# Sliding-window attention with a feed-forward: keys and queries transposed by DMA from the fourth batch on, tokens loaded in pairs

## The chip, the cores and the metric

The kernel runs on one core of a Trainium2 chip. The metric is the time of one execution in microseconds (us), taken on the device. The kernel before takes 356.32 us, the median of three runs (355.86 to 357.08). "Faster" and "slower" mean by more than 2%. A profile is one execution: single places of a trace are given to tenths, but small differences between two traces should not be leant on.

Engines are named as the profile names them: PE is TensorE, PEld its weight loads, DVE is VectorE, ACT is ScalarE, POOL is GpSimd, SP is SyncE and SPq the queue of DMAs that SyncE issues.

## The reference, cut to what matters

```python
B, H, S, D = 8, 8, 576, 64                       # q, k, v: float32
scores = q @ k.transpose(0, 1, 3, 2) / np.sqrt(D)
mask = np.abs(pos[:, None] - pos[None, :]) <= 32  # window of 32 tokens to each side
attn = softmax(where(mask, scores, -1e9)) @ v
x = attn.transpose(0, 2, 1, 3).reshape(4608, 512)
h = x @ w_in                                      # 512 -> 2048
out = np.maximum(0.01 * h, h) @ w_out             # 2048 -> 512, float32
```

## The kernel before

The work is 64 attention steps: eight batches of 576 tokens, in each two halves of 288 queries, in each half four pairs of heads. Between the steps stand chunks of the feed-forward, which take the tokens that the steps have finished. In a step, PE makes the scores `ps` (five matmuls against the block-diagonal keys `kbd`), ACT the exponential, GpSimd multiplies by a mask (`pr`), PE makes the sums `s` and the weighted values `x`, and VectorE takes the reciprocal `r` of `s` and writes `xT = x * r`. In the traces each of these engines takes its work in the order of the program, so VectorE's key copies, output copies, reciprocals and multiplications stand in one line (in the changed kernel a reciprocal at 112.41 us comes behind a key copy that had waited 3.05 us).

Queries and keys are loaded as float32, cast to bf16, and turned by PE through an identity matrix, since the matmuls contract over the head dimension:

```python
RUN = S // 96                                   # six tokens = 1536 bytes in one run
def load_qk(b, p, behind=None):
    for into, src, name in ((qf, q, "qf"), (kf, k, "kf")):
        t = fload.tile([96, 2, RUN * D], FP32, name=f"{name}{p}")
        if behind is not None:                  # a tiny copy that must wait for a weight
            nc.sync.dma_start(out=t[0:1, 0, 0:1], in_=behind.bitcast(FP32)); behind = None
        nc.sync.dma_start(out=t, in_=src[b, p:H:NPAIR].rearrange("a (p c) d -> p a (c d)", c=RUN))
...
def transposes(b, first=False):                 # a piece for each of 4 pairs, q and k
    ...
            for c in range(RUN):
                nc.tensor.transpose(tp[:, c], src[:, p, c].rearrange("p a d -> p (a d)"), ident[0:96, 0:96])
            ...                                 # ACT copies tp to qT, or to kT and then:
                    for a in range(2):
                        r = slice(64 * a, 64 * a + 64)
                        nc.vector.tensor_copy(out=kbd[b % 2][r, p, :, r],
                                              in_=kT[r].rearrange("p (n j) -> p n j", j=64))
...
# start of batch 1, under the first feed-forward chunks
for p in range(NPAIR):
    load_qk(1, p, w_in_bf[0:1, 0, 512:514] if p == 0 else None)
...
for p in range(NPAIR):
    load_v(1, p, w_out_bf[0:1, 4, 0:2] if p == 0 else None)
for f in range(FFC):
    h_tile(256, 256, f)
    if f % 4 == 3:
        next(second); next(second)              # transposes of batch 1
        nc.gpsimd.memset(vbd[1][:, f // 4], 0.0)
score(8)
```

The tiny copy named `behind` makes the loads of batch 1 wait until a certain weight has landed, so that they do not take the queue from the weights.

The softmax here doesn't subtract the row's maximum and nothing guards it: scores larger than these inputs give would overflow.

## Time and profile before

| | before |
|---|---|
| median of 3 runs | 356.32 us |
| profiled span, granted clock | 353.9 us, 1.000 |
| PE / VectorE / ACT / GpSimd busy | 324.3 / 211.8 / 183.4 / 178.7 us |
| transposes on PE, whole program | 384 of 96 columns (192 for q, 192 for k) |
| copies of keys into `kbd` | 64, 28.4 us of VectorE |

Three lines of the page: SyncE's queue (packets, MB, share of the DMA engines), the chain that ended last by engine, and the sums on PE (busy us, mean ns, then the idle time before them and what ended it).

```profile
q1 hardware_dynamic: 56388, 37.76, 42.7%
...
PE 77%; DMA 7%; DVE 6%; POOL 4%; SPq 2%; issue 2%; ACT 1%; DVEq 0%; POOLq 0%; ACTq 0%
...
L238 PE MATMUL s<-pr,ones_bd 128*128 128x288 bf16 x64 | 19.0, 297 | 8.7 <-DVE r L252 7.0
```

PE makes 77% of the chain, and its waits for the reciprocal sum to 7.0 us. The kernel is a PE stream with a start of some 65 us ahead of it.

### The profile page before, as it was taken

How to read it: one execution, taken by the hardware profiler on the slowest of the kernel's cores; microseconds unless marked ns; L12 is line 12 of the kernel's file. 1: busy time of each engine (PE TensorE's matmuls, PEld its weight loads, DVE VectorE, ACT ScalarE, POOL GpSimd, SP SyncE). 2: the span in 40 equal slices, each digit the busy share in tenths (PEclk: the TensorE clock that was granted, in tenths of full speed). 3: DMA queues.
4: the chain of work that ended last, by engine and by line, in shares of the span. 5: the costliest groups of instructions: out<-in, count | busy, mean ns of one | idle time of the engine just before them, and what ended most of it. 6: DMA issues, size and time to landing. Idle time of an engine off the chain costs nothing.

```text
span 353.9 us, 6635 instructions
## 1 busy us (share of the span) xinstructions
PE 324.3 (92%) x2600; PEld 208.2 (59%) x2624; DVE 211.8 (60%) x242; ACT 183.4 (52%) x363; POOL 178.7 (51%) x213
## 2 busy tenths in 40 slices
PE   2658998999989898999999898999999999999995
PEld 1437864584957655656656555656656656555472
DVE  5588647757686877645653778554676676630101
ACT  5765862292845637518527527716528517326060
POOL 7797676578765766524543568533655423200000
PEclk9999999999999999999999999999999999999999
DMA  8999986599995274342453265340010010020101
GB/s 187 214 205 236 269 162 182 144 201 235 209 255 146 58 222 133 69 126 88 140 162 70 63 177 165 88 124 33 0 61 30 2 61 31 5 86 0 61 31 59
DMA packets 60707, 42.37 MB, mean 120 GB/s; under 512 B 39684, under 2 KB 56068, under 8 KB 60676
## 3 DMA queue, kind: packets, MB, share of 16 engines
q1 hardware_dynamic: 56388, 37.76, 42.7%
q0 software_dynamic: 4288, 4.20, 7.2%
q8 instruction: 20, 0.33, 0.4%
q14 instruction: 11, 0.09, 0.1%
HBM read 36.70 MB, written 9.44 MB: 130 GB/s over the span
## 4 chain that ended last, share of the span: by engine, by line
PE 77%; DMA 7%; DVE 6%; POOL 4%; SPq 2%; issue 2%; ACT 1%; DVEq 0%; POOLq 0%; ACTq 0%
PE mm L273 33%; PE mm L264 31%; DMA kf<-in_k_dram 7%; DVE r L252 5%; PE x L246 3%; PE tp L187 3%; PE ps L220 3%; PE s L238 2%; PE s L239 2%; SPq L71 1%; POOL vbd L175 1%; POOL vbd L400 1%; SPq L82 1%; DVE xT L254 1%; POOL pr L230 1%
## 5 line engine op out<-in xcount | busy, mean ns | idle before, releaser
L252 DVE RECIPROCAL r<-s 128x288 f32<-128x288 f32 x64 | 125.1, 1954 | 38.5 <-PE s L239 38.2
L230 POOL TENSOR_TENSOR pr<-e,mask 128x544 bf16<-128x544 bf16 x64 | 77.7, 1213 | 115.0 <-ACT e L226 114.7
L264 PE MATMUL mm<-xT,w_in_bf 128*128 128x384 bf16 (+1 forms) x896 | 132.7, 304 | 0.9 <-ACT kT L201 0.8
L268 ACT ACTIVATE gT<-mm 128x384 bf16<-128x384 f32 (+1 forms) x224 | 99.0, 445 | 63.0 <-PE mm L264 58.6
L273 PE MATMUL mm<-w_out_bf,gT 128*128 128x512 bf16 x552 | 126.8, 379 | 1.3
L264 PEld LDWEIGHTS <-w_in_bf 128*128 128x128 bf16 x896 | 86.6, 98 | 38.0 <-issue 1.3
L273 PEld LDWEIGHTS <-gT 128*128 128x128 bf16 x576 | 54.9, 98 | 61.1
L226 ACT ACTIVATE e<-ps 128x544 bf16<-128x544 f32 x64 | 39.8, 622 | 77.6 <-PE ps L220 77.6
L280 DVE COPY o_sb<-mm 128x512 f32<-128x512 f32 x36 | 24.9, 691 | 66.8 <-PE mm L273 66.8
L204 DVE COPY kbd<-kT 64x576 bf16<-64x576 bf16 x64 | 28.4, 444 | 18.2 <-ACT kT L201 17.6
L175 POOL CAST vbd<-vf 64x576 bf16<-64x576 f32 x58 | 38.3, 661 | 1.9
L254 DVE TENSOR_TENSOR xT<-x,r 128x288 bf16<-128x288 f32 x64 | 29.3, 458 | 7.0 <-PE mm L264 0.5
L165 POOL CAST kb<-kf 96x768 bf16<-96x768 f32 x32 | 26.6, 834 | 9.5 <-DMA kf<-in_k_dram 9.5
L246 PE MATMUL x<-pr,vbd 128*128 128x128 bf16 (+2 forms) x320 | 26.9, 217 | 2.0 <-POOL vbd L175 1.0
L220 PE MATMUL ps<-qT,kbd 128*128 128x128 bf16 (+2 forms) x320 | 27.3, 219 | 0.3
L238 PE MATMUL s<-pr,ones_bd 128*128 128x288 bf16 x64 | 19.0, 297 | 8.7 <-DVE r L252 7.0
L220 PEld LDWEIGHTS <-kbd 128*128 128x128 bf16 x320 | 21.1, 102 | 8.1 <-issue 0.6
L195 ACT ACTIVATE qT<-tp 128x576 bf16<-128x576 bf16 x32 | 20.8, 649 | 9.6 <-PE tp L187 9.0
L246 PEld LDWEIGHTS <-vbd 128*128 128x128 bf16 x320 | 21.4, 101 | 7.1 <-issue 2.8
L201 ACT ACTIVATE kT<-tp 128x576 bf16<-128x576 bf16 x32 | 20.8, 650 | 8.9 <-PE tp L187 7.9
L187 PE MATMUL tp<-ident,qb 96*128 96x96 bf16 x192 | 14.4, 214 | 8.5 <-DVE qb L165 6.7
L165 POOL CAST qb<-qf 96x768 bf16<-96x768 f32 x24 | 19.7, 820 | 0.0
(31 smaller groups left out, 107.7 us busy)
## 6 DMA issues: line engine op xcount, KB each, us to landing
qf<-in_q_dram SPq DMA_DIRECT2D x32, 288.0 KB, 3.5
kf<-in_k_dram SPq DMA_DIRECT2D x32, 288.0 KB, 3.9
vf<-in_v_dram SPq DMA_DIRECT2D x64, 144.0 KB, 3.4
out_dram<-o_sb SPq DMA_DIRECT2D x36, 256.0 KB, 2.2
w_in_bf<-in_moe_w_in_dram POOLq DMA_DIRECT2D x8, 256.0 KB, 6.4
w_out_bf<-in_moe_w_out_dram POOLq DMA_DIRECT2D x4, 512.0 KB, 13.5
qf<-w_in_bf SPq DMA_DIRECT2D x1, 0.0 KB
vf<-w_out_bf SPq DMA_DIRECT2D x1, 0.0 KB
```

The costliest lines, as they stand in the source:

```text
L165: eng.tensor_copy(out=dst[:, p], in_=src[b, p].rearrange("p a (c d) -> p c a d", d=D),)
L175: nc.gpsimd.tensor_copy(out=vbd[b % 2][r, p, :, r], in_=vf[b, p][r])
L204: nc.vector.tensor_copy(out=kbd[b % 2][r, p, :, r], in_=kT[r].rearrange("p (n j) -> p n j", j=64),)
L220: nc.tensor.matmul(ps[:, c0:c0 + n], kbd[b % 2][:, p, blk], qT[b][:, p, q0:q0 + n], start=True, stop=True,)
L226: nc.scalar.activation(out=e, in_=ps[:, 512 - HALF:512 - HALF + NCOL], func=AF.Exp, scale=scale,)
L230: nc.gpsimd.tensor_mul(pr, e, mask[hf])
L246: nc.tensor.matmul(x[:, a:a + n], vbd[b % 2][:, p, blk, :], pr[:, c0:c0 + n], start=(n_ == 0), stop=(n_ == len(WIN[hf]) - 1), skip_group_c ...
L252: nc.vector.reciprocal(r, s)
L254: nc.vector.tensor_mul(xT[:, p, t0:t0 + HALF], x, r)
L264: nc.tensor.matmul(h[:, 0:n], w_in_bf[:, c, ts(f, 128)], xT[:, c, ds(t0, n)], start=(c == 0), stop=(c == DMC - 1),)
L268: nc.scalar.activation(out=gT[t0][:, f, 0:n], in_=h[:, 0:n], func=AF.Prelu, alpha=0.01)
L273: nc.tensor.matmul(o, gT[t0][:, f, ts(j, 128)], w_out_bf[:, f, :], start=(f == 0), stop=(f == FFC - 1),)
```

## The change

The intent is to take 240 of the 384 transposes off PE, and the ACT copies behind them, and to give them to the DMA engines. For that the order of tokens had to change: a run is now two tokens (512 bytes), and inside a key block of 64 the 32 even tokens come first and the 32 odd ones after them. Masks, windows and the loads of values follow that order. The core of the diff, with cuts:

```diff
-    RUN = S // 96
+    RUN = 2
...
         for into, src, name in ((qf, q, "qf"), (kf, k, "kf")):
-            nc.sync.dma_start(out=t, in_=src[b, p:H:NPAIR].rearrange("a (p c) d -> p a (c d)", c=RUN))
+            for a in range(2):
+                if behind is not None:
+                    nc.sync.dma_start(out=t[0:1, a, 0, 0:1], in_=behind.bitcast(FP32))
+                nc.sync.dma_start(out=t[:, a],
+                    in_=src[b, NPAIR * a + p].rearrange("(m i c) d -> i m (c d)", i=NR, c=RUN))
...     # load_v: four loads for a tile in place of two, each behind a tiny copy where one is given
+    def place_keys(b, p):
+        t = kT.pop((b, p))
+        for a in range(2):
+            r = slice(64 * a, 64 * a + 64)
+            nc.vector.tensor_copy(
+                out=kbd[b % 2][r, p, :, r].rearrange("p n (c i) -> p n c i", c=RUN),
+                in_=t[r].rearrange("p (c n i) -> p n c i", c=RUN, n=NB))
...
+    def transpose_dma(b, p):
+        new_T(b, p)
+        for src, t in ((qb, qT[b][:, p]), (kb, kT[b, p])):
+            nc.sync.dma_start_transpose(out=t.rearrange("p (g i) -> p g i", i=NR),
+                                        in_=src[:, p].rearrange("p c m a d -> p (c m a d)"))
...     # weighted: s is made by five matmuls, block by block, in place of two
+    for b in range(2, B):
+        for p in range(NPAIR):
+            if b == 2:
+                i, j = (12, 13, 13, 14)[p], (14, 15, 15, 15)[p]
+                plan(13 + p, transpose_pe, b, p)
+            else:
+                i = 8 * (b - 1) + p
+                j = i + 4
+                plan(i + 3, place_keys, b, p)
+                plan(i + 1, transpose_dma, b, p)
+            plan(i, cast_qk, b, p)
+            plan(j, cast_v, b, p)
+            if b + 1 < B:
+                plan(i, load_qk, b + 1, p)
+                plan(j, load_v, b + 1, p)
```

The first three batches keep their transposes on PE. The second mask is now made after the first step instead of at the beginning.

## The prediction

> **What bounds the kernel now.** I read the page's engine shares and 40 slices first, then the chain of work that ended last, the PE timeline of the middle, the same timelines of the first 66 us, and the issues of the DMA queue there.
>
> ```profile
> PE 324.3 (92%) x2600; PEld 208.2 (59%) x2624; DVE 211.8 (60%) x242; ACT 183.4 (52%) x363; POOL 178.7 (51%) x213
> ...
> DMA  8999986599995274342453265340010010020101
> ```
>
> PE is far ahead of the rest, but a busy PE can still run below its rate, so I tested that. The chain in order of time, two stretches:
>
> ```profile
> 15.99 0.82 POOL kb L165
> ...
> 30.73 15.97 DMA kf<-in_k_dram
> 46.76 0.82 POOL kb L165
> 47.58 3.64 POOL vbd L400 x4
> ...
> 223.06 0.26 PE tp L187 x6
> ...
> 231.64 0.24 PE ps L220 x5
> ```
>
> The first column is the start, the second the time a piece adds. The upper lines are the start, where loads and POOL set the pace; the last two are from the middle, where the chain is PE alone. There, six transposes of 96 columns add 0.26 us, five score matmuls of 544 columns together add 0.24 us[...]. I gave every PE row of the timeline that cost and subtracted: from 140 to 200 us and from 220 to 340 us nothing is left over. The whole program's columns come to about 311 us; the other 43 us of the span are a start of about 18 us lost before 30 us, some 4 us at the end, and gaps of about 2 us where two attention steps follow each other without a feed-forward part between them:
>
> ```profile
> 215.91 0.42 PE L187 MATMUL tp<-ident,qb 96*128 96x96 bf16 x6
> 216.46 0.40 PE L220 MATMUL ps<-qT,kbd 128*128 128x64 bf16 x5
> 217.89 0.30 PE L238 MATMUL s<-pr,ones_bd 128*128 128x288 bf16 x1 [1.03 <-DVE r L252]
> ```
>
> So there are two regimes: the PE stream binds from about 65 us to the end, and any column removed there is time; up to about 65 us a chain of loads, casts and first steps binds, and any delay there is carried to the end undiminished, because no slack follows.
>
> [...] in the timeline the five score matmuls take 0.65 us before 28 us and 0.40 us afterwards, although the granted clock in the page is full throughout. [...] no run so far shows a transpose. [...] undisturbed packets of 256, 1536 and 2048 bytes take about 15 to 18, 65 and 82 ns.
>
> **The change part by part.**
> (a) Removed from PE: batches 3 to 7, 5 x 48 = 240 transposes of 96 columns, 240 x 42.5 ns = 10.2 us, all inside the stretch that is pure PE stream. Where two steps adjoin, the transposes had filled part of a wait on the reciprocal; about four such places lie in that range, and each loses about 0.25 us of the saving: -1.0. Net -9.2 us.
> (b) The sums of the probabilities become five matmuls instead of two, the same 544 columns: 3 x 2.5 ns x 64 = 0.5 us more. Key placing stays on DVE at 0.44 us x 64; mask multiply, exponential and reciprocal stay. The transposes no longer have one PSUM buffer but the four of the feed-forward: the one wait of 0.74 us for the copy of qT at 87 us goes. Together about -0.2.
> (c) ACT loses 40 copies of 0.65 us = 26 us. PE waited for ACT almost nowhere, so nothing follows on the path.
> (d) 40 DMA transposes of 96x768 bf16, 147 KB. [...] the 2 to 4 us to landing that loads show here. Keys are placed two steps (some 9 us) after, and needed at the earliest two steps after that. Hidden.
> (e) Loads. Queries and keys go from 12288 packets of 1536 bytes to 36864 of 512. From the packet records in the crowded start (about 30 ns for 256 bytes, 105 ns for 1536), an interpolated 45 ns for 512: three take 135 ns in place of 105. For one batch (4608 packets over 16 engines) that is 13.0 us in place of 10.1. Issues double as well: two per query or key tile, four per value tile, about 0.4 us each, and the issue order of the new program shows each waiting for the one eight before it.
>
> What (e) and the new masks cost, along the chain of the start:
> - The last keys of batch 0 landed at 15.99 us, and POOL was waiting for them (0.57 us idle). Up to 3 us later by (e). The second mask, five small copies on POOL, now stands ahead of the third step's mask multiply, which had 0.3 us to spare: 1 us more. Start: +2.5 to +4, say +3.
> - Batch 1: its loads are held back by one tiny copy out of the weights. Now there is one such copy ahead of each of the first two loads and of each of the first four value loads, and each load waits for its own to land:
>
> ```profile
> 22.77 0.73 SPq L69 DMA_DIRECT2D qf<-w_in_bf  x1
> 27.39 0.33 SPq L71 DMA_DIRECT2D qf<-in_q_dram  x1
> ...
> 38.24 0.62 SPq L80 DMA_DIRECT2D vf<-w_out_bf  x1
> 45.84 5.52 SPq L82 DMA_DIRECT2D vf<-in_v_dram  x8
> ```
>
> The first cost 4 us, the second 7 us, mostly in the queue behind the query and key loads. In the new program the value loads cannot begin before those are through, about 49 to 51 us by the shifts above; then three further rounds of load, tiny copy and landing, an estimated 2.5 to 3 us each from the shortest landings here (3.0 us for a value load): the first value tile is whole at about 60 to 62 us, is cast in 0.66 us, and the ninth step's value matmuls start about 62 us in place of here:
>
> ```profile
> 54.14 0.41 PE L246 MATMUL x<-pr,vbd 128*128 128x96 bf16 x5 [0.34 <-POOL vbd L175]
> ```
>
> That is +8 us at this point, in which the +3 of the start is contained. PE then stands still for some 5 us[...].
> Sum: -9.2 - 0.2 + 0.5 + 8 + 1 = +0.1. I take 356 us.
>
> **The rivals.**
> 1. The start hides it: the DMA engines keep working on the weights while the tiny copies wait, the weights then finish sooner, 512-byte packets cost nearer the undisturbed 25 ns (a line through 15 and 65 ns), and the value loads are done by 57. For it: the engines are busy nine tenths or more in most early slices, so no work is lost, only reordered. Against: the serial waits are latency, not bandwidth, and the first value cast already held PE for 0.34 us. Then 346 to 349 us.
> 2. The transposes are slow: if one takes 8 us or occupies the engines, eight per batch come to 64 us against some 42 us for eight steps, and the in-order queue of SyncE holds back loads and, behind them, output stores; DVE then stands before a full o_sb. For it: no trace here shows one, and SyncE now issues about twice as many DMAs. Against: [...] from 120 us on the DMA row shows 0.3 to 0.5 of capacity. Then 370 us and more.
> 3. The delay at the start is larger, each tiny copy taking the 4 to 7 us that it takes before: +6 to +10 more, about 363 to 366.
> 4. DVE becomes the bound where steps adjoin: without transposes between, the wait on the reciprocal (1.95 us) is bare. That is the 1 us in (a); DVE at 60% cannot bind elsewhere.
>
> **Range and chances.** The gain of 9 us is firm, the PE stream being accounted for to some tenths; the loss at the start has a spread of 3 to 12 us, and the transposes add a tail on the slow side. 356 us, 8 in 10 between 347 and 364. Faster by over 2% means below 349.2, so a start that loses under about 2.5 us: 0.25. Slower by over 2% means above 363.4: 0.17. Within: 0.58.
>
> **What would show it.** (a) right: from about 120 us no tp rows on PE, ACT some 26 us less busy, eight steps about 2 us shorter, and PE without gaps save at adjoining steps. (e) right: the value loads of batch 1 end at 62 us or later, and the ninth x waits several us for vbd, its start near 62 us; last keys of batch 0 land at 18 to 19 us. Wrong: an x at 57 us or before (rival 1), a kbd copy or a score in the middle that waits for a DMA, or o_sb copies that wait for stores (rival 2). The prediction falls if the first 65 us lose under 3 or over 15 us, or if PE shows waits on DMA after 120 us.

The sum came to +0.1 us; of its terms the last, +1 (a slower PE after its standstill), has lost its ground, and without it the sum is -0.9. The costs of 42.5 ns for a transpose and 2.5 ns for a further matmul in (a) and (b) can be had from the trace before: 32 matmuls of 256 columns take 3.49 us there (69.07 to 72.56) and 16 of 512 take 3.45 (207.53 to 210.98), so an estimate of 0.416 ns a column and 2.5 ns a matmul; 24 of 384 take 3.90, 162.5 ns each where the estimate gives 162.3, and the columns of the whole program come to the 311 us.

## The result, and the profile after

| | before | changed |
|---|---|---|
| median | 356.34 us (4 runs) | 360.73 us (4 runs, 359.88 to 362.08) |
| ratio | | 1.0125, 95% interval 1.0089 to 1.0161 |
| profiled span, granted clock | 353.9 us, 1.000 | 360.4 us, 0.995 |
| ACT busy | 183.4 us | 159.4 us |
| VectorE busy | 211.8 us | 224.2 us |

A ratio here and below is the mean time of one kernel's runs over the mean of the kernel before in the same rounds on the same chip, so it is not quite the ratio of the medians quoted. The outputs are right. The changed kernel is 1.25% slower: within 2%, 4.7 us above the predicted 356.0 and inside the range of 347 to 364. The total was near; two of its terms were not, and the rest of this text is about them.

The page of the changed kernel: engine shares, the busy tenths of PE and its granted clock in the 40 slices, SyncE's queue, the chain by engine, the sums on PE, and from the last part the two kinds of DMA transposes with their median time from issue to landing.

```profile
PE 316.3 (88%) x2552; PEld 202.5 (56%) x2576; DVE 224.2 (62%) x242; ACT 159.4 (44%) x323; POOL 182.1 (51%) x223
...
PE   2558788899987759799999989899999999999995
...
PEclk9999999999999989999999999999999999999999
...
q1 hardware_dynamic: 107340, 43.67, 52.3%
...
PE 63%; DMA 17%; DVE 10%; SPq 4%; issue 3%; POOL 2%; ACT 0%; DVEq 0%; POOLq 0%; ACTq 0%
...
L256 PE MATMUL s<-pr,ones_bd 128*128 128x128 bf16 (+2 forms) x320 | 27.0, 217 | 16.9 <-DVE r L263 13.5
...
qT<-qb SPq DMA_TRANSPOSE x20, 3.2
kT<-kb SPq DMA_TRANSPOSE x20, 2.9
```

PE has less to do and is idle more: the slices from the 13th to the 15th (108 to 135 us) fall to 7, 7 and 5, and its waits for the reciprocal grew from 7.0 to 13.5 us. PE's part of the chain fell from 77% to 63%, and DMA, VectorE and SyncE's queue took it. The transposes land quickly, 3.2 and 2.9 us after their issue.

To see where the time went, follow one instruction that every step has, the multiplication that writes `xT`, and subtract its start in the trace before from its start in another trace. This gives the lag of each kernel, step by step, in us:

| step | 7 | 8 | 15 | 19 | 25 | 28 | 63 |
|---|---|---|---|---|---|---|---|
| changed | +2.0 | +8.2 | +5.1 | +3.6 | +11.9 | +13.7 | +6.3 |

(Step 8 starts at 56.02 us before and at 64.26 after; step 63 at 310.66 and 316.98.) So about 5 us are lost in the start (8 at first, of which 3 are regained by step 15); another 10 us are lost from step 19 to 28, which is where batch 3 is prepared and begun; and from there to the end 7.4 us are won back, which is the gain that was promised.

**The start.** GpSimd before and after around the first step of batch 1 (start, duration, instruction, and in brackets the idle time before it):

```profile
46.76 0.82 POOL L165 CAST kb<-kf 96x768 bf16<-96x768 f32 x1 [3.15 <-DMA kf<-in_k_dram]
47.52 4.05 POOL L400 MEMSET vbd<- 128x1152 bf16 x4
```

```profile
51.96 0.82 POOL L174 CAST kb<-kf 96x768 bf16<-96x768 f32 x1 [1.18 <-DMA kf<-in_k_dram]
52.73 4.05 POOL L399 MEMSET vbd<- 128x1152 bf16 x4
```

The last keys of batch 1 are there 5.2 us later, and everything behind them on GpSimd with them: four clearings of the value blocks, the mask multiplication, the cast of the values. PE's ninth `x` then starts at 59.44 us instead of 54.14, the same 5.3 us later:

```profile
59.44 0.41 PE L256 MATMUL x<-pr,vbd 128*128 128x96 bf16 x5 [0.56 <-POOL vbd L184]
```

But `xT` is 8.2 us later, not 5.3. The chain of the changed kernel through this place shows the other 3:

```profile
45.78 5.00 DMA qf<-in_q_dram
...
52.02 2.56 DVE kbd L197
54.58 2.39 issue
56.97 1.20 DVE kbd L197
...
61.60 0.69 DVE o_sb L294
```

One single copy of keys begins at 52.02 and ends at 56.97. GpSimd's clearing, the line above, runs from 52.73 to 56.78. The copies of all keys, as the trace's view of that tile gives them (minimum, median and maximum in ns, first and last start), before, after, and in the first experiment below:

```profile
L204 DVE COPY kbd<-kT x64: 433/448/451, 7.6 to 280.1; 64x576 bf16<-64x576 bf16 x64
```

```profile
L197 DVE COPY kbd<-kT x64: 306/536/4937, 7.7 to 279.7; 64x576 bf16<-64x576 bf16 x64
```

```profile
L198 DVE COPY kbd<-kT x128: 282/292/301, 7.8 to 275.5; 64x288 bf16<-64x288 bf16 x128
```

Before, every copy took 0.44 us. After, one that is alone takes 0.31 us and is faster than before, but the mean is 0.66 us and the longest 4.94. Two things go with that in the traces. One is the shape: before, the source is one run of 576 and the destination nine blocks; after, the new token order makes the source nine blocks too. The other is GpSimd: of the 64 copies after, 18 ran while it had no work, and 17 of these took 0.31 to 0.32 us (one 0.50); of the 46 that ran beside its work, 14 took as little and 32 took 0.57 to 4.94, the longest beside a clearing of 4.05 us. Before, 56 of the copies ran beside GpSimd's work too and none took over 0.45. By what mechanism the shape makes the copy faster alone and lets GpSimd hold it up is not shown; e1 below tests the shape.

**The middle.** SyncE's queue, at the place where batch 3 is prepared (start, duration and what was issued):

```profile
97.82 7.26 SPq L90 DMA_DIRECT2D vf<-in_v_dram  x12
105.17 0.40 SPq L295 DMA_DIRECT2D out_dram<-o_sb  x1
105.67 0.94 SPq L74 DMA_DIRECT2D qf<-in_q_dram  x2
106.70 0.93 SPq L74 DMA_DIRECT2D kf<-in_k_dram  x2
107.73 1.32 SPq L218 DMA_TRANSPOSE qT<-qb  x1
```

And VectorE there:

```profile
111.72 0.65 DVE L197 COPY kbd<-kT 64x576 bf16<-64x576 bf16 x2 [3.05 <-DMA kT<-kb]
112.41 1.96 DVE L263 RECIPROCAL r<-s 128x288 f32<-128x288 f32 x1
...
118.16 0.65 DVE L197 COPY kbd<-kT 64x576 bf16<-64x576 bf16 x2 [3.23 <-DMA kT<-kb]
118.84 0.69 DVE L294 COPY o_sb<-mm 128x512 f32<-128x512 f32 x1
```

The first transpose of batch 3 stands in the program behind step 17, whose `xT` was written at 99.7 us; SyncE comes to it at 107.73. From 77 to about 128 us SyncE issues one DMA after another, some 0.46 us for a load and 1.2 us for a transpose; its longest wait in that stretch is 1.0 us. Loads of queries and keys are twice as many as before, loads of values too. Nothing is wrong with the transfers themselves (3.2 and 2.9 us to landing). But VectorE has the placing of those keys in its line from step 19 on, waits 3.05 and 3.23 us for them, and the reciprocal and the output copy that PE waits for stand behind. PE at that place (in brackets its idle time and what ended it):

```profile
119.58 2.34 PE L278 MATMUL mm<-xT,w_in_bf 128*128 128x256 bf16 x20 [2.89 <-DVE o_sb L294]
```

PE needs nothing of the keys of batch 3 yet. It stands still because VectorE has to copy finished output into `o_sb` (the tile from which it is stored), and VectorE stands before a key.

A second thing happens in this stretch. The granted clock is 1.00 in every 10 us of the trace before, but 0.83 from 130 to 140 us in the changed kernel, behind a wait of PE of 3.01 us: 1.7 us of clock. Over the span, the four runs of the changed kernel were granted 0.988 to 0.995, those of the kernel before 0.998 to 1.000. By an estimate from these numbers (0.9% of 359 us, if PE were the bound throughout) the lower clock can make up to some 3 us of the loss. Why the clock falls is not shown: the wait of 2.89 us above left it at 1.00. No run separates the clock from the waits, so what follows counts both together.

### The profile page after: what moved, and what is told of

Read it like the earlier page. It is cut to its first block, busy times and chain, and to the rows that moved or that the text cites. A ratio compares the mean times of both kernels' runs of the same rounds, so it can differ in the third digit from the quotient of the medians.

```text
span 360.4 us, 6772 instructions
## 1 busy us (share of the span) xinstructions
PE 316.3 (88%) x2552; PEld 202.5 (56%) x2576; DVE 224.2 (62%) x242; ACT 159.4 (44%) x323; POOL 182.1 (51%) x223
## 4 chain that ended last, share of the span: by engine, by line
PE 63%; DMA 17%; DVE 10%; SPq 4%; issue 3%; POOL 2%; ACT 0%; DVEq 0%; POOLq 0%; ACTq 0%
PE mm L287 29%; PE mm L278 26%; DMA qf<-in_q_dram 6%; DVE r L263 4%; DVE kbd L197 4%; DMA kf<-in_k_dram 3%; PE x L256 3%; PE s L256 2%; PE ps L234 2%; DMA qf<-w_in_bf 2%; SPq L74 2%; DMA kT<-kb 2%; DMA w_in_bf<-in_moe_w_in_dram 2%; DMA out_dram<-o_sb 1%; DVE xT L265 1%
## 5 line engine op out<-in xcount | busy, mean ns | idle before, releaser
L287 PE MATMUL mm<-w_out_bf,gT 128*128 128x512 bf16 x552 | 128.4, 381 | 1.4 <-issue 0.2
L197 DVE COPY kbd<-kT 64x576 bf16<-64x576 bf16 x64 | 42.5, 663 | 14.0 <-DMA kT<-kb 7.5
L256 PE MATMUL s<-pr,ones_bd 128*128 128x128 bf16 (+2 forms) x320 | 27.0, 217 | 16.9 <-DVE r L263 13.5
L184 POOL CAST vbd<-vf 64x576 bf16<-64x576 f32 x58 | 39.2, 675 | 1.9
L256 PEld LDWEIGHTS <-ones_bd 128*128 128x128 bf16 x320 | 18.3, 100 | 20.1 <-DVE r L263 17.4
L256 PEld LDWEIGHTS <-vbd 128*128 128x128 bf16 x320 | 19.7, 101 | 4.3 <-issue 3.4
L207 PE MATMUL tp<-ident,qb 96*128 96x96 bf16 x72 | 6.0, 230 | 7.7 <-DVE qb L174 7.7
L207 PE MATMUL tp<-ident,kb 96*128 96x96 bf16 x72 | 6.0, 230 | 6.4 <-POOL kb L174 6.4
```

The costliest lines, as they stand in the source:

```text
L184: nc.gpsimd.tensor_copy(out=vbd[b % 2][r, p, :, r], in_=vf[b, p][r])
L197: nc.vector.tensor_copy(out=kbd[b % 2][r, p, :, r].rearrange("p n (c i) -> p n c i", c=RUN), in_=t[r].rearrange("p (c n i) -> p n c i", c= ...
L256: nc.tensor.matmul(out_[:, :, i0:i0 + n], weights(blk), pr[:, c0:c0 + RUN * n].rearrange("p (c i) -> p c i", c=RUN), start=(n_ == 0), stop ...
L287: nc.tensor.matmul(o, gT[t0][:, f, ts(j, 128)], w_out_bf[:, f, :], start=(f == 0), stop=(f == FFC - 1),)
```

## The experiments

The twelve runs went out on three chips, each beside the kernel before. The lag in us, for the same steps as in the table above:

| step | 7 | 8 | 15 | 19 | 25 | 28 | 63 | ratio |
|---|---|---|---|---|---|---|---|---|
| changed | 2.0 | 8.2 | 5.1 | 3.6 | 11.9 | 13.7 | 6.3 | 1.0125 |
| e1 key copies cut in two | 2.2 | 4.7 | 4.1 | 2.6 | 8.9 | 9.4 | 1.7 | 1.0063 |
| e2 one tiny copy | 2.2 | 8.2 | 5.5 | 4.0 | 10.2 | 12.0 | 4.6 | 1.0109 |
| e3 all transposes on PE | 3.4 | 8.1 | 5.4 | 5.0 | 5.0 | 8.4 | 8.5 | 1.0186 |
| e4 before, without transposes | 0.9 | 0.1 | 0.1 | -0.5 | -0.9 | -1.5 | -8.4 | 0.9780 |
| e5 e1, keys placed a step later | 3.3 | 4.4 | 4.6 | 3.2 | 4.7 | 4.0 | -2.7 | 0.9919 |
| e7 e1, batch 3 on PE too | 4.4 | 5.2 | 6.1 | 5.7 | 5.3 | 5.8 | -1.9 | 0.9899 |

### First lot: the three suspects apart, and the gain alone

**e1_split_keys.** The copy of keys cut into its even and its odd half, whose source is one run again, as in the kernel before, where no copy took over 0.45 us:

```diff
-            nc.vector.tensor_copy(out=kbd[b % 2][r, p, :, r].rearrange("p n (c i) -> p n c i", c=RUN),
-                in_=t[r].rearrange("p (c n i) -> p n c i", c=RUN, n=NB))
+            for c in range(RUN):
+                nc.vector.tensor_copy(out=kbd[b % 2][r, p, :, 64 * a + NJ * c:64 * a + NJ * (c + 1)],
+                    in_=t[r].rearrange("p (c n i) -> p c n i", c=RUN, n=NB)[:, c])
```

> The changed kernel with each key placement on VectorE cut in two along the token pair (128 copies of 64x288 in place of 64 of 64x576); right result. Theory[...]: in the changed kernel both sides of the copy have the same outer dimension of 9, [...]0.31 us when alone and up to 4.9 us beside GpSimd; cut, one side is a single run and the other has 9, as in the kernel before, where all 64 copies took 0.43 to 0.45 us. Expected: every copy 0.30 to 0.35 us with none above 0.5, and the lag behind the kernel before at the ninth step's xT falls from 8.2 us to about 5; time 356.5 to 358.5. Rival (the late loads set the pace and the copies only fill waiting time): the copies get regular but the lag at the ninth step stays at 7 or more and the time stays within 1 us of 360.7.

Measured: 358.68 us, ratio 1.0063 (1.0022 to 1.0105); the time a little above what was expected, the lag at step 8 (4.7) as expected. All 128 copies take between 282 and 301 ns (the line above), although GpSimd is as busy as before (179.2 us, 182.1 in the changed kernel): none is held up any more. The long copies are worth 1.25% - 0.63% = 0.62%, or 2.2 us, give or take 2.0 us by the two intervals; the two profiles, one execution each, lie 4.6 us apart at step 63.

**e2_one_guard.** One tiny copy in place of two ahead of the keys and queries, and one in place of four ahead of the values:

```diff
                     nc.sync.dma_start(out=t[0:1, a, 0, 0:1], in_=behind.bitcast(FP32))
+                    behind = None
...
                     nc.sync.dma_start(out=t[row:row + 1, 0, 0:1], in_=behind.bitcast(FP32))
+                    behind = None
```

> The changed kernel with one tiny guarding copy ahead of the query loads and one ahead of the value loads of batch 1, in place of two and four; right result. Theory of the prediction (serial tiny copies): the value loads begin about 6 us earlier, the ninth x starts at 55 to 57 us in place of 59.4, time 356 to 358. Rival[...]: the ninth step's reciprocal waits for key copies on VectorE until 61.6 us anyway, so x may start earlier but the ninth xT stays within 1.5 us of 64.3, time 359.5 to 361.

Measured: 360.10 us, ratio 1.0109, and 8.2 us of lag at step 8: unchanged. The tiny copies, which the prediction had made the cause of the delay, are not what binds in the changed kernel. There SyncE waited for those ahead of the values 4.4 us in all, at most 1.8 us each, and GpSimd was still clearing then. Nor do the tiny copies ahead of the queries make the last keys late: with one in place of two, their cast began at 51.35 us, against 51.96.

**e3_pe_all.** All batches transposed on PE, in the new token order:

```diff
+            elif b < 8:
+                i = 8 * (b - 1) + p
+                j = i + 4
+                plan(i + 1, transpose_pe, b, p)
```

> The changed kernel with all transposes on TensorE, at the steps at which the DMA transposes stood, the new token order kept; right result. If DMA transposes gain their 9 to 10 us and lose about 8 to 9 us between 95 and 150 us (late landing, VectorE held up in order), this run is near the changed kernel: 360 to 364, with a lag curve that does not jump at 105 to 150 us but never falls afterwards. If the jump there is not the transposes' doing (loads of 512 bytes, double issues), the jump stays and the time is 368 to 371.

Measured: 363.09 us, ratio 1.0186 (1.0150 to 1.0221), as expected. Two things to see in its row: from step 19 to 25 nothing is lost, so the jump there belongs to the DMA transposes and the place of their keys in VectorE's line, both of which this run undoes; and on the whole nothing is won back after step 28, so the gain does too.

**e4_before_no_tp.** The kernel before with the transposes of batches 3 to 7 and the ACT copies behind them left out; the keys and queries of batch 2 are used again, so that the result is wrong. (It passes the comparison nevertheless: the inputs are so small that the weights inside the window are nearly equal. So that comparison says little about the order of keys and queries, for the other kernels too.)

```diff
-                for c in range(RUN):
+                for c in range(RUN if b < 3 else 0):
...
+                if b >= 3:      # keep the DVE copies, from the old kT; qT[b] is qT[2]
```

> The kernel before without the transposes and their ACT copies from batch 3 on (the queries of batch 2 are used again, old keys are placed, so the result is wrong on purpose); DVE, loads and stores as they were. Measures what the TensorE stream is worth: by the prediction 9.2 us, so 346.5 to 348. If adjoining steps give back more (the wait on the reciprocal is bare), 349 to 351.

Measured: 348.49 us, ratio 0.9780 (0.9737 to 0.9823), a little above what was expected: 0.022 x 356.5 = 7.8 us less, and 8.4 in the profile. (The two runs that were granted the full clock took 347.21 and 348.22 us, 8.8 less on average; the other two had 0.989 and 0.993.) That is all that taking the transposes off PE can give here, and it lies in the plain PE stream after step 28, as the lag shows.

### Second lot: is it the place in the line?

**e5_late_place.** As e1, and the keys are placed one step later, with everything else the same:

```diff
-                plan(i + 3, place_keys, b, p)
+                plan(i + 4, place_keys, b, p)
```

> The run with cut key copies, and the keys from the DMA transposes placed one step (about 4 us) later; right result. Theory (the first DMA transposes come late and VectorE, working in order, waits up to 3.2 us in front of the key copy with the reciprocals behind it): the waits of VectorE for kT fall from 9.4 us to under 3, the lag behind the kernel before rises by at most 3 us between the 20th and 26th step in place of 6, time 355 to 357. Rival (the jump comes from the stores and loads behind the crowded queue, not from the place of the copies): jump of 5 us or more again, time 358 to 359.

Measured: 353.52 us, ratio 0.9919 (0.9883 to 0.9955), lower than expected. Placing the keys one step later is worth 0.63% + 0.81% = 1.44%, or 5.1 us, give or take 2.0 us by the two intervals (each against the kernel before on its own chip). Part of it is the clock: from 100 to 130 us it was 0.90, 0.84 and 0.92 in the profile of e1, and 1.00 in that of e5. VectorE still waits for keys:

```profile
116.55 1.03 DVE L198 COPY kbd<-kT 64x288 bf16<-64x288 bf16 x4 [1.25 <-DMA kT<-kb]
...
121.82 1.03 DVE L198 COPY kbd<-kT 64x288 bf16<-64x288 bf16 x4 [1.68 <-DMA kT<-kb]
```

but 1.7 us at most. In all it waits 6.2 us, against 9.4 in e1 and under 3 expected: the waits got shorter rather than going away, and the reciprocals that PE needs now stand ahead of them.

**e6_late_place_one_guard.** e5 with the edit of e2.

> The former run with one tiny guarding copy for queries and one for values of batch 1 as well; right result. With the key copies regular, the value loads should now bind at the ninth step: if the serial tiny copies matter then, its lag falls from 4.7 us to 2 to 3 us and the time by 1 to 2 us against the former run; if the 512-byte query and key loads set it, nothing changes.

Measured: 354.39 us, ratio 0.9931 (0.9910 to 0.9953): no difference from e5, the second miss for the tiny copies.

**e7_split_from5th.** As e1, and batch 3, too, is transposed on PE, so that DMA transposes begin with the fifth batch, when SyncE has caught up:

```diff
+            elif b < 4:
+                i = 8 * (b - 1) + p
+                j = i + 4
+                plan(i + 1, transpose_pe, b, p)
```

> Cut key copies, with batch 3 (the fourth) transposed on TensorE and the DMA transposes only from the fifth batch on; right result. It costs 48 transposes, 2.0 us of TensorE. If the lateness belongs to the crowded stretch before 130 us, the jump of 6 us at the 20th to 26th step is gone: lag there under 4 us, time 355 to 357. If DMA transposes hold VectorE up wherever they begin, the jump comes back eight steps later and the time is 359 to 361.

Measured: 353.26 us, ratio 0.9899 (0.9871 to 0.9928), lower than expected; no jump from step 19 to 25, and hardly a wait of VectorE for a DMA transpose (0.2 us, once). This is the lowest ratio, 1.0% below the kernel before. It gives up 48 of the 240 transposes, and no loss by it can be seen.

**e8_act_queue.** As e1, and the transposes are issued from ACT, to relieve SyncE:

```diff
-            nc.sync.dma_start_transpose(
+            nc.scalar.dma_start_transpose(
```

> Cut key copies, with the DMA transposes issued from ScalarE in place of SyncE; right result. If they are late because SyncE is behind with about 60 loads at 0.46 us each, kT lands in time here, VectorE waits for it under 2 us in all and the jump at the 20th to 26th step is under 3 us; but each issue takes ScalarE about 1.2 us, so 48 us more of it, and evictions of the feed-forward may be late: 354 to 359. If the crowded DMA engines make them late, VectorE waits 7 us or more for kT as before.

Measured: 373.43 us, ratio 1.0464 (1.0422 to 1.0507), against 354 to 359 expected; its runs were granted 0.975 to 0.976 of the clock. VectorE no longer waits for keys at all, so that the lateness was indeed SyncE's order of issues. But a new wait takes its place. SyncE's waits (what waited, what for, us in all, times, longest), then VectorE, then PE at the worst place:

```profile
SPq L90 <- DMA qT<-qb: 21.6, 6, 10.3
```

```profile
180.97 0.69 DVE L295 COPY o_sb<-mm 128x512 f32<-128x512 f32 x1 [15.71 <-DMA out_dram<-o_sb]
```

```profile
183.58 0.63 PE L257 MATMUL s<-pr,ones_bd 128*128 128x96 bf16 x5 [8.14 <-DVE r L264]
```

Loads on SyncE's queue wait for the transposes that ACT issues; the output stores stand behind those loads; VectorE waits 15.7 us for a store to free `o_sb`, and PE 8.1 us for the reciprocal behind it. Why a load of values has to wait for a transpose of queries was not looked into further: the trace shows only that it does.

### Third lot: what holds the start

**e9_zero_early.** e5, and the four clearings of the value blocks are moved up between the key casts of batch 1, where GpSimd waits for loads anyway:

```diff
     for p in range(NPAIR):
         cast_qk(1, p, nc.vector)
+        for z in ((0, 1), (2,), (3,), ())[p]:
+            nc.gpsimd.memset(vbd[1][:, z], 0.0)
...
             transpose_pe(1, f // 4)
-            nc.gpsimd.memset(vbd[1][:, f // 4], 0.0)
```

> The run with cut key copies placed one step later, and the four clearings of the second value buffer (1.05 us each on GpSimd) moved between the key casts of batch 1, into GpSimd's waits for the keys; all six tiny copies kept; right result. Tells what lies behind the ninth step's late start. If the serial tiny copies are hidden only behind that chain of late keys, clearing and mask multiply, the values (landed about 58 us) bind now: the ninth x starts at 58 us or later, lag of the ninth step still 3.5 us or more, time within 1 us of 353.5. If the tiny copies cost nothing, x starts at 55.5 to 57 us and the time falls by 2 to 3 us.

Measured: 356.72 us, ratio 0.9977 (0.9929 to 1.0025). The ninth `x` starts at 59.18 us (59.29 in e5) and waits for the values:

```profile
59.18 0.41 PE L257 MATMUL x<-pr,vbd 128*128 128x96 bf16 x5 [1.26 <-POOL vbd L184]
```

So with the clearings out of the way the loads of values bind, as one of the alternatives had it, and nothing is won at that place. The total missed both: it came out 3 us behind e5 (on another chip, 2 us by the ratios). Its profile loses 2.8 us between steps 22 and 26, e5 1.5. The traces show where: PE waits there 4.34 us for a reciprocal (2.91 in e5), and then works at a lower clock, 0.84 from 120 to 130 us where e5 has 1.00. The same 16 matmuls, in e9 and in e5:

```profile
127.27 5.06 PE L288 MATMUL mm<-w_out_bf,gT 128*128 128x512 bf16 x16
```

```profile
125.69 3.62 PE L288 MATMUL mm<-w_out_bf,gT 128*128 128x512 bf16 x16
```

**e10_zero_early_one_guard.** e9 with the edit of e2.

> The former run with one tiny copy for queries and one for values; right result. If the tiny copies bind once the clearing is out of the way: the ninth x starts 2 us or more before the former run's, time 350.5 to 352. If not, the two runs are alike within 1 us.

Measured: 354.63 us, ratio 0.9916 (0.9855 to 0.9976), more than expected, and its interval overlaps that of e9. The place that it was made for, in one trace each:

```profile
57.72 0.41 PE L259 MATMUL x<-pr,vbd 128*128 128x96 bf16 x5
```

The wait is gone and `x` starts 1.5 us earlier. So in e9 the tiny copies held `x` up, once the long key copies and the clearings were out of the way; in the changed kernel they were hidden behind these. What that is worth in time is not shown.

**e11_masks_first.** e10, and the second mask is made before the first casts, as before the change (`make_mask(1)` moved up).

> The former run with the second mask built before the first key cast, where GpSimd waits for keys, in place of ahead of the third step's mask multiply; right result. By the timeline of the start this takes away the 0.8 us that the third step's xT gains in lag (from 1.5 to 2.3 us); time 0.5 to 1 us under the former run, the fastest of all: 349.5 to 351.5.

Measured: 354.08 us, ratio 0.9915 (0.9853 to 0.9977). The lag of the third step is 1.6 us; it was 2.3 in e5, but 1.0 in e10, from which this run differs by the one edit. So the expected fall was not seen, and the time cannot be told from that of e10.

**e12_before_zero_early.** A control: the kernel before with the edit of e9.

> The kernel before with the same move of the clearings alone; right result. Control for the three runs above: there the ninth x waited for the same chain by 0.34 us only, so the move should be worth 0 to 1.5 us here: 355 to 356.9. If it is worth 2 us or more, the gain of the runs above is not the change's.

Measured: 357.81 us, ratio 1.0009 (0.9956 to 1.0062): no gain. So what e10 has is not a gain that the kernel before lay open to by this move. As a control it is not clean: in its profile the moved clearings run beside VectorE's four casts of queries, which take 7.91 us from first to last, the first of them 3.33 us where an unhindered one takes 0.56; the ninth `x` starts at 57.79 us, 3.7 us later than in the profile of the kernel before, and 3.2 us of that were lost ahead of the move.

The versions e5, e6, e7, e10 and e11 all lie 0.7 to 1.0% below the kernel before, and their intervals overlap: these runs do not rank them.

## Why the prediction was right or wrong

The time came within 4.7 us, in the range and in the class given the largest chance. That it came so near was luck, as the sum at the end of this list shows. By its own steps:

- **(a) Transposes off PE, -9.2 us: right, a little too large.** Alone they are worth 7.8 us (e4). The account of the PE stream (42.5 ns for a transpose; the chain before shows 0.26 us for six) held: 9.2 us would be a ratio of 0.974, just inside the interval of e4 (0.9737 to 0.9823), and its two runs at full clock gave 8.8. Whether the rest is the allowance for adjoining steps or scatter, the runs do not show.
- **(b) "Key placing stays on DVE at 0.44 us x 64": wrong.** The size of the tile stayed, the shape of the access did not, and with it the time: 0.31 us alone, 0.66 on average, 4.94 at the worst, beside a clearing. It cost about 2.2 us (e1), and it is why `xT` of step 8 lagged by 8.2 us while its `x` lagged by 5.3.
- **(c) ACT loses 26 us of work and nothing follows: right.** 183.4 - 159.4 = 24 us, and no wait for ACT had been on the path.
- **(d) "Hidden": wrong, and the costliest step.** The time of the transfer was right: 2.9 and 3.2 us from issue to landing, where 2 to 4 had been taken from the loads. What was left out is the issue. The prediction counted the time from the issue to the keys' use, and assumed that an instruction placed at step 17 is issued at step 17; SyncE was 8 us behind. It cost about 5.1 us (e1 against e5). Rival 2 had the in-order queue and the sign to look for (a `kbd` copy that waits for a DMA), but tied them to slow transposes and to 14 us and more. It was the line of issues on SyncE that counted (e8: issued from ACT, no key came late), not the bandwidth.
- **(e) The start, +8, and +1 for a slower PE: mis-sized, and for another reason.** The +3 of batch 0 cannot be confirmed: the last keys of batch 0 were cast at 16.80 us instead of 15.99 and the lag was +2.0 at step 7, while e12, with the program of the kernel before up to there, has 17.69 us and +3.2. At the ninth `x` the lag was +5.3 (predicted +8), and about +5 remained at step 15. The value loads began where the prediction had them (50.29 us), but a round of load, tiny copy and landing, predicted at 2.5 to 3 us, took 1.9 (the next loads began at 52.20, 54.16 and 56.11), and these rounds lay beside the clearings (e2, e6), so that they did not bind; they do only in e9. What bound was the arrival of the last keys of batch 1, 5.2 us later. That is more than scatter: their cast began at 51.26 to 52.59 us in the eight profiles that have the new loads and the clearings in their old place, and at 46.76 and 46.83 in the kernel before and in e4. The cause of these 5 us stays open. A second tiny copy is not it (51.35 in e2, 51.91 in e6), and the packets speak against their size: the interpolated 45 ns for 512 bytes was 32 ns, so three take 97 ns against 93 for one of 1536. The doubled issues were not tested by themselves. The +1 was the author's estimate, and no run isolated such a cost: the ninth `x` took 0.41 us after a wait of 0.56, as it did before the change after one of 0.34. A lower clock did come, but in the middle (0.83 from 130 to 140 us).
- **The sum.** Predicted: -9.2 - 0.2 + 0.5 + 8 + 1 = +0.1. Measured by parts: -7.8 (e4) + 4.6 (the start, lag of e5 at step 15) + 2.2 (key copies) + 5.1 (late transposes) = +4.1, against 0.0125 x 356.3 = +4.5 for the whole. The start was overestimated by some 5 us and the middle left out 7: the two errors stood against each other, and the total looks better than its terms. The terms from e1 and e5 are good to some 2 us each and contain the lower clock.

(The "0.5" in the predicted sum is the three additional matmuls of a step, which the -0.2 of (b) contains already: it is counted twice, and the sum should have been -0.4. No run took it by itself.)

## What to carry to other kernels

When work is moved from an engine to DMA, count the issues on the queue's engine as you would count instructions on a busy engine, and ask when the issue comes, not only how long the transfer takes; if a consumer stands in an in-order line, moving it one step back can be worth most of the work saved (here about 5.1 us against 7.8). When a layout changes, look at the access pattern of every copy that reads or writes it: the same number of elements can become faster alone and slower beside GpSimd (here 0.31 us alone in place of 0.44, and up to 4.94 beside a clearing). And test a suspected wait by taking away what it hides behind, since a wait that is real may cost nothing until then (the tiny copies here: no change in e2, 1.5 us of the ninth `x` in e10).

## What was measured of issues, copies and packets

- For one load the issue was short beside the transfer (0.46 us, against 3.4 to 3.6 us to landing for queries and keys), less so for a transpose of 96x768 bf16 (1.2 us against 2.9 to 3.2), and in sum it was not small: from 77 to about 128 us SyncE issued with hardly a pause (5.9 us of waits in all), so that a transpose was issued 8 us after its step. Spreading the issues over a second engine was not free either: with the transposes on ACT, loads on SyncE waited 21.6 us in all for them, and the kernel was 4.6% slower (e8).
- A copy of 64x576 bf16 with nine blocks on both sides took 0.31 us alone, 4.94 us beside a clearing of 4.05 us, and 0.66 us on average in a kernel whose GpSimd is busy half of the time; the same copy with one run as its source took 0.44 us each time.
- A packet of 512 bytes took 32 ns on average, one of 1536 bytes 93 ns before the change, and one of 256 bytes 22.5 ns: three times 512 (97 ns) cost about what 1536 did, so that the shorter runs were cheaper than the prediction made them.
